# Shared Winograd sums carried from PSUM bank to PSUM bank by ScalarE instead of added by VectorE

## The chip, the cores and the metric

The kernel runs on one core of a Trainium2 chip. The engines that matter are TensorE (PE in the profile; PEld is its weight load), VectorE (DVE), ScalarE (ACT), GpSimd (POOL) and the DMA queue that SyncE (SP) feeds. The metric is device time in microseconds (us) of one execution.

## The reference

Attention with a block mask feeds a soft mixture of eight experts, which feeds a second network. The change lies in the mixture:

```python
for e in range(E):                       # E = 8, x is 2304 x 512
    h = np.maximum(x @ w1[e], 0.0)       # w1[e] is 512 x 1024
    ye = h @ w2[e]                       # w2[e] is 1024 x 512
    out += P[:, e:e + 1] * ye            # P from eight rounds of row and column scaling
```

Attention before it and the last network (matrix product, softmax, layer norm, matrix product) after it are the same in both kernels.

## The kernel before

Attention runs from the start to about 380 us, with expert 0 filled in between; the row and column scaling follows, and from 461 us the other seven experts run as fourteen units `u` = 2 to 15 (half an expert each). They run three times, for three blocks of 768 tokens. In **pass 0** (461 to 905 us) each unit's weights are also scaled, split into f16 high and low parts by ACT (high) and POOL (low) and stored; the second layer (`second_layer`) is a plain product. In **passes 1 and 2** (905 to 1690 us) the stored weights are read back, and the second layer (`second_products`) uses seven products as well. The last network runs from 1690 us to the end.

Every first layer (`first_layer`, 42 of them: 14 units in 3 passes) multiplies 2x2 blocks by Winograd's scheme: seven products 1 to 7, each for two halves `g` = 0, 1 of the hidden features. One product (`product`, L823 to L825) is six matmuls of 128x384 that accumulate in one PSUM bank. Bank a of a half takes products 1 and 2, bank b takes 6, 7 and 4, bank c takes 5 and 3. Sums that several outputs share are made outside PE: ACT copies product 1 out of bank a to SBUF (`r1`, L849), and DVE adds (`plus`, L835): u2 = b + r1 after product 6, u3 = b + r1 after 7, vu3 = c + u3 after 5, b + r1 in place after 4, and c + u2 in place after 3. Each finished output goes to `hidden`: in pass 0 ACT (L868) and DVE (L869) make the high and low parts of its ReLU, in passes 1 and 2 one DVE instruction (L880) makes the weighted ReLU into `hb`. From `hb`, ACT casts (`hf`, L887) and POOL subtracts (L888 the low part, L891 `minus` the differences; one `minus` of a unit runs on DVE), which feed the second products (`yps<-hf`). Results are added into `acc` by DVE (L935 in passes 1 and 2, L987 in pass 0).

First-layer banks and most of the second products' banks come from one pool of six (`l1p`); the second layer of pass 0 and every fourth second product use another pool of two (`mm`). A matmul that begins a bank's reuse waits until the engine that reads the old content is done. Two small matmuls, the squared norms of a coming unit's weights (`bound`, L488) and the steps of a table (`gate_table`, L523 to L544), write into unused columns of a first-layer bank (`aside`). A scheduler lays out each engine's order at build time from the program; at run time each engine works its list in that order.

## Time and profile before

| | |
|---|---|
| median of 3 runs | 1930.81 us (1930.1 to 1933.39) |
| profiled execution, its own time | 1930.03 us |
| span of its trace | 1928.1 us |
| PE busy over the span | 1815.9 us (94%) |
| DVE busy | 1469.4 us (76%) |
| ACT busy | 857.2 us (44%) |
| POOL busy | 1083.8 us (56%) |

The own time is the span plus 1.93 us around it. Busy times are sums over stages whose limits differ, so the two stages with first layers are read by themselves below. In rows of waits, the engine and line before the arrow waited, those behind it ended the wait; the numbers are us in total, times, and the longest in us. A matmul's recorded 0.33 us overlaps the next one's.

### The profile page before, as it was taken

To read this page: it belongs to the slowest core of one execution; us is meant where nothing else is said; L and a number is where in the kernel's file an instruction comes from. 1 tells how busy PE (TensorE), PEld (TensorE's weight loads), DVE (VectorE), ACT (ScalarE), POOL (GpSimd) and SP (SyncE) were. 2 spreads that over 40 slices of the span, in tenths; PEclk is the share of its full clock that TensorE was granted. 3 is DMA by queue.
4 is the path that set the end of the run, shared out by engine and by line. 5 is a ranking of instruction groups with operands and counts; after the bars stand their busy time and mean duration, and the time that the engine had idled before them with its cause. 6 is when DMAs were issued, how large, how long until landed. Compare 5 with 4: busy or idle time off the path is not lost.

```text
span 1928.1 us, 31148 instructions
## 1 busy us (share of the span) xinstructions
PE 1815.9 (94%) x10520; PEld 1218.5 (63%) x10520; DVE 1469.4 (76%) x3267; ACT 857.2 (44%) x1723; POOL 1083.8 (56%) x914
## 2 busy tenths in 40 slices
PE   4799999979999999999999999999999999999999
PEld 4688998877544454444566555665665555568887
DVE  6878777676787766676688788777778888889774
ACT  5676666574876757552422212223221221233332
POOL 7675655255777565651766747769564775841000
PEclk9899999989999999999999999999999999999999
DMA  8665645255585564452655555555555555451100
GB/s 230 160 173 141 172 128 163 83 178 160 201 269 191 199 202 162 148 196 67 200 178 156 171 166 161 158 144 179 164 158 177 157 169 169 157 205 49 39 23 33
DMA packets 191710, 300.47 MB, mean 156 GB/s; under 512 B 19760, under 2 KB 77760, under 8 KB 189632
## 3 DMA queue, kind: packets, MB, share of 16 engines
q1 hardware_dynamic: 191552, 298.49, 50.1%
q8 instruction: 84, 1.38, 0.3%
q14 instruction: 74, 0.61, 0.1%
HBM read 192.96 MB, written 77.14 MB: 140 GB/s over the span
## 4 chain that ended last, share of the span: by engine, by line
PE 39%; DVE 5%; POOL 3%; DMA 2%; issue 2%; ACT 0%; SPq 0%; DVEq 0%; POOLq 0%; ACTq 0%
PE yps L823 5%; PE yps L825 5%; PE yps L824 5%; PE psb L823 2%; PE psb L825 2%; PE psb L824 2%; PE ops L1290 2%; PE ops L1292 2%; PE ops L1291 2%; POOL hf L888 2%; PE h L1237 2%; PE h L1238 2%; PE h L1239 2%; PE psc L825 1%; PE psc L824 1%
## 5 line engine op out<-in xcount | busy, mean ns | idle before, releaser
L888 POOL TENSOR_TENSOR hf<-hb,hf 128x768 f16<-128x768 f32 x196 | 332.0, 1715 | 114.8 <-ACT hf L887 106.5
L887 ACT CAST hf<-hb 128x768 f16<-128x768 f32 x196 | 156.5, 830 | 331.8 <-POOL hb L891 130.2
L824 PEld LDWEIGHTS <-W 128*128 128x128 f16 x1960 | 192.5, 98 | 169.3 <-issue 43.8
L825 PEld LDWEIGHTS <-W 128*128 128x128 f16 x1960 | 192.7, 98 | 132.7 <-POOL W L554 3.0
L823 PEld LDWEIGHTS <-W 128*128 128x128 f16 x1960 | 192.5, 98 | 132.6 <-issue 3.6
L823 PE MATMUL yps<-hf,W 128*128 128x384 f16 x784 | 255.4, 326 | 1.8 <-POOL hf L888 1.7
L824 PE MATMUL yps<-hf,W 128*128 128x384 f16 x784 | 255.8, 326 | 0.0
L825 PE MATMUL yps<-hf,W 128*128 128x384 f16 x784 | 255.6, 326 | 0.0
L935 DVE SCALAR_TENSOR_TENSOR acc<-yps,rscw,acc 128x384 f32<-128x384 f32 x364 | 213.2, 608 | 14.4 <-PE yps L825 14.2
L823 PE MATMUL psb<-X,W 128*128 128x384 f16 x504 | 166.0, 329 | 12.0 <-DVE u L835 8.6
L825 PE MATMUL psb<-X,W 128*128 128x384 f16 x504 | 166.0, 330 | 0.7 <-POOL W L554 0.7
L824 PE MATMUL psb<-X,W 128*128 128x384 f16 x504 | 166.1, 330 | 0.0
L554 POOL TENSOR_TENSOR W<-raw,W 128x512 f16<-128x512 f32 x84 | 99.8, 1206 | 112.6 <-ACT W L553 108.4
L891 POOL TENSOR_TENSOR hb<-hb 128x768 f32<-128x768 f32 x84 | 155.6, 1852 | 5.9 <-DVE hb L880 5.4
L245 POOL TENSOR_SCALAR e<-e,sv 128x128 f32<-128x128 f32 (+2 forms) x144 | 82.9, 578 | 98.9 <-DVE sv L241 30.5
L981 PE MATMUL yps<-w,h 128*128 128x512 f16 x336 | 128.3, 382 | 10.7 <-DVE acc L987 9.5
L835 DVE TENSOR_TENSOR u<-psb,r 128x384 f32<-128x384 f32 x168 | 90.6, 551 | 60.0 <-PE psb L825 26.7
L554 POOL TENSOR_TENSOR w<-raw,w 128x512 f16<-128x512 f32 (+1 forms) x96 | 121.4, 1283 | 25.2 <-ACT w L553 24.9
L982 PE MATMUL yps<-w,h 128*128 128x512 f16 x336 | 128.2, 381 | 0.0
L983 PE MATMUL yps<-w,h 128*128 128x512 f16 x336 | 128.1, 381 | 0.0
L823 PE MATMUL psc<-X,W 128*128 128x384 f16 x336 | 110.2, 328 | 11.9 <-DVE acc L935 5.1
L1274 POOL TENSOR_SCALAR lh<-ln 128x1024 f16<-128x1024 f32 x18 | 19.1, 1062 | 176.9 <-DVE rs L1247 65.0
(262 smaller groups left out, 4700.4 us busy)
## 6 DMA issues: line engine op xcount, KB each, us to landing
W<-fd SPq DMA_DIRECT2D x392, 256.0 KB, 3.0
fd<-W SPq DMA_DIRECT2D x154, 256.0 KB, 2.2
raw<-in_w1s SPq DMA_DIRECT2D x14, 1024.0 KB, 6.1
raw<-in_w SPq DMA_DIRECT2D x14, 1024.0 KB, 7.4
fd<-w SPq DMA_DIRECT2D x84, 128.0 KB, 2.5
raw<-in_w SPq DMA_DIRECT2D x40, 256.0 KB, 3.6
kh<-khigh SPq DMA_DIRECT2D x64, 144.0 KB, 2.6
kl<-kraw SPq DMA_DIRECT2D x64, 144.0 KB, 2.7
```

Of the source, the lines that this page charges most:

```text
L554: nc.gpsimd.tensor_tensor(t[:, 1, :], raw, full(t[:, 0, :]), op=ALU.subtract)
L823: nc.tensor.matmul(ps, wh, xl, start=start and kc == 0, stop=False, skip_group_check=True)
L824: nc.tensor.matmul(ps, wh, xh, start=False, stop=False, skip_group_check=True)
L825: nc.tensor.matmul(ps, wl, xh, start=False, stop=stop and kc == 1, skip_group_check=True)
L835: nc.vector.tensor_tensor(to, bank[g, a], tmp[g, "r1" if a == "b" else name[1:]], op=ALU.add)
L887: nc.scalar.copy(hi, a)
L888: nc.gpsimd.tensor_tensor(lo, a, hi, op=ALU.subtract)
L891: eng.tensor_tensor(o, a, b, op=ALU.subtract)
L935: nc.vector.scalar_tensor_tensor(a, ps, r, a, op0=ALU.mult, op1=ALU.add)
L981: nc.tensor.matmul(ps, hl, ws[c][:, 0, :], start=c == 0, stop=False)
L982: nc.tensor.matmul(ps, hh, ws[c][:, 1, :], start=False, stop=False)
L983: nc.tensor.matmul(ps, hh, ws[c][:, 0, :], start=False, stop=c == 3)
```

## The change

Bank b of a half now begins as a copy of product 1: after product 1 ACT copies bank a into bank b (PSUM to PSUM), and products 6, 7 and 4 accumulate onto it, without a first matmul that clears. Bank b then holds u2 after product 6 and u3 after product 7, so ACT copies it out to SBUF twice, and after product 4 it is the finished output. DVE keeps only vu3 = c + u3 and c + u2. The products are issued in a written-out order in which the two halves alternate (1, 1, 5, 5, 6, 6, 2, 7, 2, 7, 4, 3, 4, 3). Since accumulation onto copied data needs banks that a matmul has written before, six matmuls write the six banks once before pass 0, and a chain of six one-column DVE instructions reads them. The steps of the table move to the two-bank pool, behind the first layer, and `bound` moves from behind product 5 to behind product 4 of the first half.

```diff
@@ -483,9 +483,9 @@
             if pin:
                 tc.keep_in_program_order(ins)
 
-    def bound(u, ps):
-
-        nc.tensor.matmul(ps, ones, norms.pop(u), start=True, stop=True)
+    def bound(u, ps, fresh=False):
+
+        nc.tensor.matmul(ps, ones, norms.pop(u), start=fresh, stop=True, skip_group_check=True)
         halved(tw[:, u, :], ps)
         k = powers[u] = sml.tile([P, 2], U32, tag="pw", name="pw")
         nc.vector.tensor_scalar(k, tw[:, u, :], -1.0, float(W1B + 189), op0=ALU.mult, op1=ALU.add)
@@ -515,19 +515,17 @@
         nc.vector.tensor_scalar_mul(w, pr[:, :, u // 2], rsc[:, u : u + 1])
         return w
 
-    table_bank = [None]
-
     def gate_table():
 
         gm = const.tile([P, 1], F32, name="pgm")
         nc.vector.tensor_reduce(gm, pr, axis=AX.XY, op=ALU.max)
         yield
-        pt = table_bank[0][:, BLK:512]
+        pt = mm.tile([P, 512], F32, tag="mm", name="pt")
         nc.tensor.transpose(pt[0:1, 0:P], gm, ident)
         g1 = const.tile([1, 1], F32, name="pg1")
         nc.vector.tensor_reduce(g1, pt[0:1, 0:P], axis=AX.X, op=ALU.max)
         yield
-        pb = table_bank[0][:, BLK:512]
+        pb = mm.tile([P, 512], F32, tag="mm", name="pt")
         nc.tensor.matmul(pb[:, 0:1], ones[0:1, :], g1, start=True, stop=True)
         k = const.tile([P, 1], U32, name="pk")
         c = const.tile([P, 1], U32, name="pc")
@@ -540,7 +538,7 @@
         yield
         pv = const.tile([P, P], F32, name="prt")
         for a, n in ((0, P), (P, NT * E - P)):
-            pt = table_bank[0][:, BLK:512]
+            pt = mm.tile([P, 512], F32, tag="mm", name="pt")
             nc.tensor.transpose(pt[0:n, 0:P], prs.rearrange("p t e -> p (t e)")[:, a : a + n], ident)
             nc.scalar.copy(pv[0:n], pt[0:n, 0:P])
             nc.sync.dma_start(pdram.rearrange("t e p -> (t e) p")[a : a + n], pv[0:n])
@@ -692,7 +690,7 @@
 
 
 
-    PRODUCTS = "1627543"
+    PRODUCTS = "1562743"
 
     SECOND = "3175624"
 
@@ -829,38 +827,43 @@
         bank, whole = {}, {}
         tmp = {}
 
-        def plus(g, name, a, to=None):
-            if to is None:
-                to = tmp[g, name] = tmpp.tile([P, BLK], F32, tag=name, name=name)
-            nc.vector.tensor_tensor(to, bank[g, a], tmp[g, "r1" if a == "b" else name[1:]], op=ALU.add)
+        def take(g, a):
+            whole[g, a] = l1p.tile([P, 512], F32, tag="l1", name=f"ps{a}")
+            bank[g, a] = whole[g, a][:, 0:BLK]
+
+        def plus(g, name, a, to):
+            nc.vector.tensor_tensor(to, bank[g, a], tmp[g, name], op=ALU.add)
             return to
 
-
-        plan = (("1", "a"), ("6", "b"), ("2", "a"), ("7", "b"), ("5", "c"), ("4", "b"), ("3", "c"))
-        for i, a in plan:
-            start, stop = i in "165", i in "243"
-            for g in range(2):
-                if start:
-                    whole[g, a] = l1p.tile([P, 512], F32, tag="l1", name=f"ps{a}")
-                    bank[g, a] = whole[g, a][:, 0:BLK]
-                product(W[i], X[i], bank[g, a], g, start, stop)
-                if i == "1":
-                    t = tmp[g, "r1"] = tmpp.tile([P, BLK], F32, tag="r1", name="r1")
-                    nc.scalar.copy(t, bank[g, "a"])
-                elif i == "6":
-                    plus(g, "u2", "b")
-                elif i == "2":
-                    hidden(g, 1, 1, bank[g, "a"])
-                elif i == "7":
-                    plus(g, "u3", "b")
-                elif i == "5":
-                    hidden(g, 2, 2, plus(g, "vu3", "c"))
-                elif i == "4":
-                    hidden(g, 2, 1, plus(g, "v", "b", bank[g, "b"]))
-                else:
-                    hidden(g, 1, 2, plus(g, "vu2", "c", bank[g, "c"]))
-            if i == "5" and aside:
-                aside(whole[0, "a"], whole[1, "a"])
+        def part(name):
+            return tmpp.tile([P, BLK], F32, tag=name, name=name)
+
+        plan = (
+            ("1", 0), ("1", 1), ("5", 0), ("5", 1), ("6", 0), ("6", 1), ("2", 0),
+            ("7", 0), ("2", 1), ("7", 1), ("4", 0), ("3", 0), ("4", 1), ("3", 1),
+        )
+        banks = {"1": "a", "2": "a", "6": "b", "7": "b", "4": "b", "5": "c", "3": "c"}
+        for i, g in plan:
+            a = banks[i]
+            if i in "15":
+                take(g, a)
+            product(W[i], X[i], bank[g, a], g, i in "15", i in "243")
+            if i == "1":
+                take(g, "b")
+                nc.scalar.copy(bank[g, "b"], bank[g, "a"])
+            elif i in "67":
+                t = tmp[g, "u2" if i == "6" else "u3"] = part("u2" if i == "6" else "u3")
+                nc.scalar.copy(t, bank[g, "b"])
+                if i == "7":
+                    hidden(g, 2, 2, plus(g, "u3", "c", part("vu3")))
+            elif i == "2":
+                hidden(g, 1, 1, bank[g, "a"])
+            elif i == "4":
+                hidden(g, 2, 1, bank[g, "b"])
+            elif i == "3":
+                hidden(g, 1, 2, plus(g, "u2", "c", bank[g, "c"]))
+            if (i, g) == ("4", 0) and aside:
+                aside(whole[1, "a"])
 
     def plain_hidden(hs):
         def hidden(g, i, j, src):
@@ -1075,7 +1078,7 @@
             norm(2)
             norm(3)
             for w in (2, 3):
-                bound(w, mm.tile([P, 512], F32, tag="mm", name="tot")[:, 0:2])
+                bound(w, mm.tile([P, 512], F32, tag="mm", name="tot")[:, 0:2], True)
         if i == 3:
             scale(2)
         if i == 4:
@@ -1086,6 +1089,13 @@
         while cost < 20:
             cost += next(begun, 20)
     run(begun)
+    fill6 = [l1p.tile([P, 512], F32, tag="l1", name="fill") for _ in range(6)]
+    for t in fill6:
+        nc.tensor.matmul(t[:, 0:BLK], ident16, X["1"][:, 0, 0, :], start=True, stop=True)
+    z = const.tile([P, 1], F32, name="z")
+    nc.vector.tensor_copy(z, fill6.pop()[:, 0:1])
+    while fill6:
+        nc.vector.tensor_tensor(z, fill6.pop()[:, 0:1], z, op=ALU.add)
     xctx.close()
     ectx = ExitStack()
     dec = ectx.enter_context(tc.tile_pool(name="dec", bufs=1, side="left"))
@@ -1123,17 +1133,16 @@
     for u in range(2, 16):
         hs = {}
 
-        def aside(first, second):
+        def aside(bank):
             for i, w in enumerate({2: (), 3: (4, 5)}.get(u, (u + 2,))):
                 if w < 16:
-                    bound(w, second[:, BLK + 2 * i : BLK + 2 * i + 2])
-            if 3 < u < 9:
-                table_bank[0] = first
-                next(table)
+                    bound(w, bank[:, BLK + 2 * i : BLK + 2 * i + 2])
 
         if u < 13:
             fetch(u + 3)
         first_layer(W, X, plain_hidden(hs), aside)
+        if 3 < u < 9:
+            next(table)
         if before:
             second_layer(*before)
         if u == 3:
```

The three places below are from the same first layer (pass 2, the eighth unit). A name such as psb_16746 is a tile with its number; the halves have their own tiles (before: psa_16728, psb_16746, psc_16795 for half 0; psa_16737 and psb_16755 for half 1. After: psa_16611, psb_16618, psc_16629 for half 0; psa_16620 and psb_16627 for half 1).

On PE, the first matmul of most products and of the second products between them (X1 is the input of product 1, and so on; a product is twelve rows, six weight loads and six matmuls), before:

```order
L823 MATMUL psa_16728<-X1_13157,W_16700 128x384
...
L823 MATMUL psa_16737<-X1_13157,W_16700 128x384
...
L823 MATMUL psb_16746<-X6_13158,W_16702 128x384
...
L823 MATMUL psb_16755<-X6_13158,W_16702 128x384
...
L823 MATMUL psc_16795<-X5_13161,W_16708 128x384
...
L823 MATMUL psa_16728<-X2_13159,W_16704 128x384
...
L823 MATMUL psb_16746<-X7_13160,W_16706 128x384
...
L823 MATMUL yps_16867<-hf_16578,W_16714 128x384
...
L823 MATMUL psb_16746<-X4_13162,W_16710 128x384
...
L823 MATMUL psc_16795<-X3_13163,W_16712 128x384
...
L824 MATMUL yps_16875<-hf_16578,W_16714 128x384
```

and with the change:

```order
L821 MATMUL psa_16611<-X1_13084,W_16583 128x384
...
L821 MATMUL yps_16773<-hf_16480,W_16599 128x384
...
L821 MATMUL psa_16620<-X1_13084,W_16583 128x384
...
L821 MATMUL psb_16618<-X6_13086,W_16587 128x384
...
L821 MATMUL psa_16611<-X2_13087,W_16589 128x384
...
L821 MATMUL psc_16629<-X5_13085,W_16585 128x384
...
L821 MATMUL psb_16618<-X7_13088,W_16591 128x384
...
L821 MATMUL yps_16746<-hf_16461,W_16597 128x384
...
L821 MATMUL psb_16618<-X4_13089,W_16593 128x384
...
L821 MATMUL psc_16629<-X3_13090,W_16595 128x384
...
L821 MATMUL yps_16754<-hf_16461,W_16597 128x384
...
L821 MATMUL psc_16636<-X3_13090,W_16595 128x384
```

Product 6 of half 0 (psb_16618 from X6) stands two groups of six matmuls behind the end of product 1 of that half, and the second product yps_16754, which takes the next bank in turn, the b bank of half 0, begins six matmuls after that bank's product 4 (psb_16618 from X4) has ended.

On ACT, the copies between the casts, before:

```order
L887 CAST hf_16373<-hb_16194 128x768
L887 CAST hf_16578<-hb_16448 128x768
L887 CAST hf_16597<-hb_16482 128x768
L553 CAST w32_16529<-f64_16539 128x256
L849 COPY r1_16735<-psa_16728 128x384
L849 COPY r1_16744<-psa_16737 128x384
L553 CAST w32_16546<-f64_16556 128x256
L887 CAST hf_16618<-hb_16616 128x768
L887 CAST hf_16638<-hb_16501 128x768
L887 CAST hf_16658<-hb_16482 128x768
```

and with the change:

```order
L890 CAST hf_16480<-hb_16359 128x768
L551 CAST w32_16412<-f64_16422 128x256
L853 COPY psb_16618<-psa_16611 128x384
L551 CAST w32_16429<-f64_16439 128x256
L853 COPY psb_16627<-psa_16620 128x384
L890 CAST hf_16501<-hb_16499 128x768
L856 COPY u2_16649<-psb_16618 128x384
L890 CAST hf_16521<-hb_16385 128x768
L856 COPY u2_16657<-psb_16627 128x384
L856 COPY u3_16673<-psb_16618 128x384
L890 CAST hf_16541<-hb_16359 128x768
L890 CAST hf_16560<-hb_16394 128x768
```

Two copies have become six, and they stand singly between casts of `hf` and of `w32` (the decoding of late weights), which come from POOL's and DVE's results.

On DVE, from the end of a decoding step on, before:

```order
L835 TENSOR_TENSOR u2_16753<-psb_16746,r1_16735 128x384
L835 TENSOR_TENSOR u2_16762<-psb_16755,r1_16744 128x384
L880 SCALAR_TENSOR_TENSOR hb_16770<-psa_16728,pb_16404 128x384
L880 SCALAR_TENSOR_TENSOR hb_16770<-psa_16737,pb_16404 128x384
L835 TENSOR_TENSOR u3_16785<-psb_16746,r1_16735 128x384
L835 TENSOR_TENSOR u3_16793<-psb_16755,r1_16744 128x384
L835 TENSOR_TENSOR vu3_16802<-psc_16795,u3_16785 128x384
L880 SCALAR_TENSOR_TENSOR hb_16804<-vu3_16802,pb_16404 128x384
L835 TENSOR_TENSOR vu3_16813<-psc_16806,u3_16793 128x384
L935 SCALAR_TENSOR_TENSOR acc_109<-yps_16867,rscw_106,acc_109 128x384
L880 SCALAR_TENSOR_TENSOR hb_16804<-vu3_16813,pb_16404 128x384
L835 TENSOR_TENSOR psb_16746<-psb_16746,r1_16735 128x384
```

and with the change:

```order
L883 SCALAR_TENSOR_TENSOR hb_16665<-psa_16611,pb_16291 128x384
L835 TENSOR_TENSOR vu3_16675<-psc_16629,u3_16673 128x384
L883 SCALAR_TENSOR_TENSOR hb_16665<-psa_16620,pb_16291 128x384
L883 SCALAR_TENSOR_TENSOR hb_16677<-vu3_16675,pb_16291 128x384
L938 SCALAR_TENSOR_TENSOR acc_109<-yps_16746,rscw_106,acc_109 128x384
L835 TENSOR_TENSOR vu3_16694<-psc_16636,u3_16692 128x384
L883 SCALAR_TENSOR_TENSOR hb_16703<-psb_16618,pb_16291 128x384
L883 SCALAR_TENSOR_TENSOR hb_16677<-vu3_16694,pb_16291 128x384
L835 TENSOR_TENSOR psc_16629<-psc_16629,u2_16649 128x384
L883 SCALAR_TENSOR_TENSOR hb_16712<-psc_16629,pb_16291 128x384
L894 TENSOR_TENSOR hb_16394<-hb_16394,hb_16359 128x768
L938 SCALAR_TENSOR_TENSOR acc_109<-yps_16754,rscw_106,acc_109 128x384
```

The two u2, two u3 and the two in-place additions on psb have gone; the weighted ReLU of psb_16618 stands behind vu3 of the other half.

## Rows read from the trace of the kernel before

**Rows 1.** The page: span, then busy us (share) and instructions of each engine.

```profile
span 1928.1 us, 31148 instructions
PE 1815.9 (94%) x10520; PEld 1218.5 (63%) x10520; DVE 1469.4 (76%) x3267; ACT 857.2 (44%) x1723; POOL 1083.8 (56%) x914
```

**Rows 2.** Windows: stretch, its us, busy of each engine, TensorE clock, DMA.

```profile
461.00:905.00 444.00, 417.54 (x2202) 216.91 (x2201) 329.92 (x587) 289.80 (x519) 265.92 (x217) 0.98 0.57 189
905.00:1690.00 785.00, 764.27 (x4635) 454.21 (x4634) 629.06 (x1131) 202.88 (x309) 515.98 (x317) 1.00 0.54 166
```

**Rows 3.** Waits of PE in pass 0 (461 to 905 us).

```profile
PE yps L981 <- DVE acc L987: 9.5, 10, 2.6
PE psc L823 <- DVE vu L835: 4.6, 6, 1.2
PE psa L531 <- DVE h L869: 2.6, 1, 2.6
PE psc L823 <- DVE h L869: 2.2, 1, 2.2
PE psa L825 <- POOL W L554: 1.5, 1, 1.5
```

**Rows 4.** Waits of PE in passes 1 and 2 (905 to 1690 us).

```profile
PE psb L823 <- DVE u L835: 7.6, 3, 3.7
PE psc L823 <- DVE acc L935: 5.1, 5, 1.8
PE psa L823 <- DVE acc L935: 2.3, 7, 0.5
PE psb L823 <- DVE acc L935: 2.0, 1, 2.0
PE psa L823 <- ACT r L849: 1.8, 5, 0.5
PE yps L823 <- POOL hf L888: 1.7, 1, 1.7
```

**Rows 5.** Windows of four stretches after long waits of PE, columns as in Rows 2.

```profile
540.00:600.00 60.00, 54.03 (x266) 27.63 (x264) 46.66 (x81) 42.66 (x76) 47.99 (x38) 0.91 0.71 236
660.00:670.00 10.00, 7.41 (x30) 3.10 (x28) 7.74 (x15) 10.00 (x18) 4.65 (x5) 0.83 0.53 164
1325.00:1345.00 20.00, 17.56 (x96) 9.93 (x96) 17.39 (x22) 6.93 (x12) 17.70 (x10) 0.91 0.60 197
1635.00:1645.00 10.00, 6.70 (x31) 3.62 (x31) 8.03 (x16) 2.72 (x5) 6.64 (x5) 0.83 0.47 137
```

**Rows 6.** Groups by line: the additions that go, and the copy.

```profile
L835 DVE TENSOR_TENSOR u<-psb,r 128x384 f32<-128x384 f32 x168 | 90.6, 551 | 60.0 <-PE psb L825 26.7 <-ACT r L849 25.4 <-ACT hf L887 7.4
L835 DVE TENSOR_TENSOR psb<-psb,r 128x384 f32<-128x384 f32 x84 | 46.4, 555 | 1.0 <-PE psb L825 0.8
L849 ACT COPY r<-psa 128x384 f32<-128x384 f32 x84 | 38.7, 477 | 34.6 <-PE psa L825 32.2 <-issue 2.3
```

**Rows 7.** Timeline of PE, two matmuls in a row (start, us).

```profile
1316.11 0.33 PE L824 MATMUL psa<-X,W 128*128 128x384 f16 x1
1316.27 0.33 PE L825 MATMUL psa<-X,W 128*128 128x384 f16 x1
```

**Rows 8.** Timeline of ACT: the copy after the matmul of Rows 7.

```profile
1316.69 0.48 ACT L849 COPY r<-psa 128x384 f32<-128x384 f32 x1 [2.83 <-PE psa L825]
```

**Rows 9.** Timeline of PE: the last matmul of another layer's product 1.

```profile
1006.31 0.33 PE L825 MATMUL psa<-X,W 128*128 128x384 f16 x1
```

**Rows 10.** Timeline of ACT behind it (idle before, and what ended it).

```profile
1009.37 0.83 ACT L887 CAST hf<-hb 128x768 f16<-128x768 f32 x1 [1.88 <-POOL hb L891]
1010.11 0.85 ACT L849 COPY r<-psa 128x384 f32<-128x384 f32 x2
```

**Rows 11.** Waits of ACT over the span: casts for POOL's differences.

```profile
ACT hf L887 <- POOL hb L891: 130.2, 58, 5.6
```

**Rows 12.** Timeline of DVE where pass 0 begins.

```profile
458.90 2.12 DVE L687 TENSOR_TENSOR y<-yps,y 128x384 f32<-128x384 f32 x4 [4.10 <-PE yps L680]
```

## The prediction

> **What bounds the kernel now.** I read the page first, then windows for the two stages that have first layers, then PE's waits in each, then the timeline at the places the change touches. Over the span PE is busy 94% [rows 1]; TensorE is the bound, and the change does not touch its matmuls. So nothing is won by freeing DVE as such: a gain can come only from time in which PE stands still. The windows give that time [rows 2]: in pass 0 PE is busy 417.5 of 444 us (26.5 idle), in passes 1 and 2 764.3 of 785 (20.7 idle). DVE is busy 74% and 80% there, ACT 65% and 26%. PE's waits say what ended the idle time. In pass 0 it is nearly always DVE [rows 3]: 9.5 us for `acc` (a bank of the two-bank pool not yet read), 4.6 for vu3, 2.2 for the c bank's old content, 2.6 for a table step that waits for the ReLU that still reads its bank. In passes 1 and 2 it is u (7.6 us in three waits) and `acc` (9.4 in three groups) [rows 4].
>
> A long wait costs twice. In the windows around the longest waits the granted clock is 0.91 and 0.83 [rows 5], that is, some matmuls after the wait run at the lower of the two levels, 1.2 in place of 2.4 GHz. The time lost is (1 - clock) times the window: 60 x 0.09 = 5.4, 10 x 0.17 = 1.7, 20 x 0.09 = 1.8, 10 x 0.17 = 1.7, together 10.6 us. Idle time and clock make 47.2 + 10.6 = 57.8 us: the ceiling of any gain in these stages.
>
> **What goes.** The 168 additions for u2 and u3 and the 84 in place on bank b: 90.6 + 46.4 = 137 us of DVE work [rows 6], 3.3 us in each of 42 first layers. ACT gets four more copies per layer (six for two), 168 x 0.477 = 80 us [rows 6]. No row shows an ACT copy from PSUM into PSUM. Its nearest rows are the copy to SBUF (0.477) and DVE's pair, which costs 0.551 into SBUF and 0.555 into PSUM: where the result goes makes no difference there. I take 0.48 and hold 0.55 possible; since the copy matters only by whether it beats the next product, 0.07 us changes no term below. (The Trainium skill, ScalarE: Activation LUTs, Step-by-step: what each stage is for, says that ScalarE writes PSUM with less latency than SBUF; by that the copy would be a little shorter and the sum the same. No run here shows it yet.)
>
> Pass 0. The waits for vu3 go: vu3 had to follow product 5 and, on a busy DVE, u3; now product 5 is early (60 matmuls ahead of product 3 of its half, where it was some 25), and one copy on ACT and one addition on DVE must fit between products 7 and 3, some 30 matmuls or 5 us apart in the new order: -4.6. The c bank is no longer taken behind DVE's backlog: -2.2. The table's matmuls leave the bank that ReLUs read: -2.6. The 9.5 us for `acc` are DVE's backlog of up to 2.6 us; 3.3 us of work per layer leave its queue, but not all stand ahead of the late `acc`, and the two-bank pool stays: I take half, -4.7 (bounds 0 and 9.5). The clock comes back where its wait goes: all of the 5.4 (the table's and the c bank's waits lie there) and half of the 1.7 after an `acc` wait: -6.2. Sum 20.3.
>
> Passes 1 and 2. The u waits go: product 7 now follows copies that ACT makes, and the two long waits (3.5 and 3.7 us) came while DVE was held by its own other work. -7.6, and the clock behind them, 1.8 + 1.7 = -3.5. Of 9.4 us for `acc` I take a third, -3.1, because the six banks are taken earlier in the new order. Sum 14.2.
>
> The 1.5 us for POOL's W, 1.7 for `hf` and 1.8 for ACT's r stay.
>
> **What comes.** First, a start-up: the six bank-writing matmuls need the banks of the last `yps`, whose four additions on DVE take 2.12 us from 458.90 on [rows 12], and the first product then waits for the chain of one-column reads. PE used to work through this stretch on products 1 and 6, 16 matmuls of 0.16 us [rows 7], 2.6 us. The next units' weights are late there anyway (the 1.5 us for W), which hides part: +2 (bounds 0 and 4).
>
> Second, ACT is now in PE's way. Undisturbed, a copy begins 0.42 us after the start of product 1's last matmul [rows 7, 8] and lasts 0.48: 0.9 us. In the layer shown, product 6 of the first half begins 13 matmuls after that start, 2.1 us; 1.2 to spare. In other layers there is more, 24 matmuls, and in pass 0 whole groups of second-layer matmuls stand between, which makes it 4 us and more in nearly all layers. But ACT is busy 65% there [rows 2], with 289.8 / 14 = 21 us of in-order work per layer and now 2 more, so some copies will come late: an estimate of 0.2 us per layer, +3 (bounds 0 and 10). In passes 1 and 2 the copy stands behind casts of `hf` that wait for POOL. One such case of before: product 1's last matmul starts at 1006.31 [rows 9], the cast waits 1.88 us for POOL until 1009.37, and the copy begins at 1010.11 [rows 10], 3.8 us behind instead of 0.42. Before, nothing but DVE's u noticed. Now product 6 would stand 4.3 - 2.1 = 2.2 us. Such waits are 58 in all, 2.2 us each [rows 11], two in each of the 28 layers. Also, the b bank of the first half is given to a second product six matmuls (1 us) after its product 4, while its ReLU on DVE (0.55) stands behind vu3 of the other half, which waits for a copy: no slack at all. If one layer in five is hit for the full 2.2 us, that is 0.4 us per layer, 28 x 0.4 = +11.2 (bounds 0 and 51, below).
>
> **Sum.** -20.3 - 14.2 + 2 + 3 + 11.2 = -18.3. The profiled execution took 1930.03 us, 0.8 below the median of the runs, which is nothing. 1930.0 - 18.3 = 1911.7, so 1912. The `acc` terms may give 8 us less or 11 more, the start-up 2 either way, the copies may cost 6 more or 11 less; as these hardly all fall to one side, I hold 13 us either way for this case: 1899 to 1925.
>
> **Rivals.** (A) *ACT's queue becomes the bound of the passes*: slower. If every layer of passes 1 and 2 has a copy behind a cast that waits 2.2 us for POOL and runs 0.83, less 1.2 to spare, it loses 1.8 us, 28 x 1.8 = 51; with 34.5 gained and 5 lost elsewhere that is +22, 1952. It decides against the change from (34.5 - 5) / 28 = 1.1 us per layer on. For it: 58 such waits, and single copies between casts in the new ACT order. Against it: in some layers of before the copy followed the matmul at once, as in rows 8; and when PE has once stood still, POOL catches up. (The Trainium skill, TensorE: Matmul & The Clock Gate, Architectural detail, says that ScalarE's and VectorE's queues are strictly first in, first out, and that PE pulls only weight loads ahead; so a blocked cast holds the copy and then every matmul behind product 6. Rows 10 agree, 3.8 us against 0.42.)
>
> (B) *The waits only move.* DVE stays late for `acc` and the b bank, and what u and vu3 gave is waited for there: the terms of "what goes" shrink to those for the table, c bank and clock of pass 0 (about 11) and the new ones eat them: 1930, no change. For it: `acc` is the largest wait already.
>
> (C) *All goes*: waits of DVE vanish whole and the copies are never late. 57.8 less the 5.0 that stay and 2 for the start-up is 51: 1879. For it: DVE falls from 74 to about 64% in pass 0.
>
> **Chances.** Forecast 0.62, A 0.18, B 0.12, C 0.08. A difference of 0.2% (3.9 us) is about what can be told from none; so faster 0.71 (forecast and C, with a little of the forecast's edge gone to no change and A), same 0.12, slower 0.17. The range that leaves out the far half of A and most of C is 1886 to 1942; the forecast's own is 1899 to 1925.
>
> **What would show it.** In the profile after: L835 down from 420 instructions (five per half and layer) to 168, L849's copies up from 84 to 252 at about 0.48 us; PE idle in pass 0 near 13 us in place of 26.5, with no wait for vu3 or in the table; in passes 1 and 2 no wait for u, and new rows of PE's psb waiting for ACT's copies, about 0.4 us per layer. A shows as such waits of 30 us and more in total; B as `acc` and ReLU waits that have grown. I would be wrong by the size of one term above all, the lateness of ACT's copies, which the order cannot tell.

## The result and the profile after

The changed kernel takes **1950.1 us** (median of 4 runs, 1947.28 to 1953.98) against 1930.45 of the kernel before beside it (1930.1 to 1933.39): ratio 1.0099, 95% interval 1.0087 to 1.0111. It is 1% slower where 1912 us and faster were forecast, and 1950 lies outside the range. The profiled execution took 1950.32 us, 20.3 more than that of before.

The page first, in the columns of [rows 1]:

```profile
span 1948.5 us, 30887 instructions
PE 1818.8 (93%) x10526; PEld 1221.0 (63%) x10526; DVE 1359.3 (70%) x3021; ACT 926.8 (48%) x1891; POOL 1088.5 (56%) x914
```

DVE is busy for 110 us less (137 us of additions left it) and ACT for 70 us more (80 us of copies came); PE's own work has hardly moved (1815.9 to 1818.8). So the 20 us are time in which PE stands still or runs at a lower clock. Four stages, cut at fixed events on PE's timeline (the last matmul of the row and column scaling, the last one of pass 0's second layer, the last second product, the last matmul of all), tell where:

| us | up to pass 0 | pass 0 | passes 1 and 2 | last network |
|---|---|---|---|---|
| before | 443.2 | 475.3 | 783.2 | 222.1 |
| after | 447.3 | 476.3 | 799.5 | 221.2 |
| difference | +4.1 | +1.0 | +16.3 | -0.9 |

The first stage holds the same work in both. Over all the kernels below it lasted 442.1 to 447.3 us, with the kernels that share its code on both ends, so +4.1 is the spread from one execution to the next and no effect of the change. What the change did is +1.0 in pass 0, where -15.3 was forecast (-20.3 + 2 + 3), and +16.3 in the passes, where -3.0 was (-14.2 + 11.2).

PE's waits after, first in pass 0 (461 to 905 us), to be held against [rows 3]:

```profile
PE yps L984 <- DVE acc L990: 11.2, 5, 3.2
PE psa L488 <- DVE h L872: 7.1, 5, 1.8
PE psc L821 <- DVE vu L835: 4.3, 3, 1.9
PE psa L821 <- DVE h L872: 2.2, 1, 2.2
PE psb L821 <- ACT u L856: 1.8, 2, 1.5
PE psb L821 <- ACT psb L853: 1.3, 1, 1.3
```

`acc` and vu3, which should have shrunk, stand where they were (9.5 and 4.6 before). The copies cost what was put down for them (3.1 us). New are 7.1 us in which `bound` (L488) waits for a ReLU. Then passes 1 and 2 (905 to 1690 us), to be held against [rows 4]:

```profile
PE psb L821 <- ACT psb L853: 11.1, 8, 3.0
PE yps L821 <- DVE acc L938: 6.9, 4, 2.4
PE yps L821 <- DVE hb L883: 4.0, 3, 2.1
PE psa L821 <- DVE acc L938: 3.9, 1, 3.9
PE yps L821 <- POOL hf L891: 3.0, 2, 2.0
PE psb L821 <- ACT u L856: 2.7, 3, 1.2
PE psc L821 <- DVE acc L938: 1.7, 2, 1.0
PE psc L821 <- DVE vu L835: 0.2, 1, 0.2
```

The u waits on DVE are gone (7.6 before). But `acc` waits are 12.5 us (9.4 before), `hb` is new with 4.0, and ACT's copies add 13.8. These rows sum to 33.5 us, those of [rows 4] to 20.5: +13.0. The clock adds the rest: summed over windows of 10 us from 915 to 1715, (1 - granted clock) times 10 us was 3.4 us before and 6.8 after. 13.0 + 3.4 = 16.4, the 16.3 of the table. In pass 0 (445 to 915) PE's idle time went from 26.5 to 29.5 us and the clock's loss from 6.8 to 5.1: +1.3, near the +1.0 of the table.

One late copy, in the passes. PE's timeline, the last matmul of product 1 and the first of product 6 (start, us, what it waited for):

```profile
1682.10 0.33 PE L823 MATMUL psa<-X,W 128*128 128x384 f16 x1
1685.07 0.32 PE L821 MATMUL psb<-X,W 128*128 128x384 f16 x1 [2.64 <-ACT psb L853]
```

and ACT's between the two:

```profile
1683.81 0.83 ACT L890 CAST hf<-hb 128x768 f16<-128x768 f32 x1 [1.88 <-POOL hb L894]
1684.55 0.85 ACT L853 COPY psb<-psa 128x384 f32<-128x384 f32 x2
```

ACT was free when product 1 ended, but the cast at the head of its list waited 1.88 us for POOL's difference, and the copies of both halves stood behind it. This is rival A's mechanism; it cost 8 waits, where A counted one in each of 28 layers.

`bound`, in pass 0: DVE's timeline ahead of the matmul, then PE's.

```profile
819.73 1.17 DVE L811 TENSOR_TENSOR raw<-s,raw 128x512 f32<-128x512 f32 x1
820.83 1.50 DVE L872 SCALAR_TENSOR_TENSOR h<-vu,h 128x384 f16<-128x384 f32 x1
822.26 0.55 DVE L872 SCALAR_TENSOR_TENSOR h<-psa,h 128x384 f16<-128x384 f32 x1
```

```profile
822.86 0.38 PE L488 MATMUL psa<-wq,ones 128*128 128x2 f32 x2 [1.82 <-DVE h L872]
```

A matmul of two columns holds PE for 1.82 us, because it writes beside bank a of half 1 and the ReLU that reads that bank stands in DVE's list behind a sum of the next unit's weights and another ReLU.

The groups by line, beside [rows 6]:

```profile
L835 DVE TENSOR_TENSOR vu<-psc,u 128x384 f32<-128x384 f32 x84 | 46.4, 553 | 94.1 <-ACT u L856 94.1
L856 ACT COPY u<-psb 128x384 f32<-128x384 f32 x168 | 78.4, 475 | 86.4 <-PE psb L823 86.0
L853 ACT COPY psb<-psa 128x384 f32<-128x384 f32 x84 | 39.0, 468 | 44.0 <-PE psa L823 41.4 <-DVE h L872 2.6
```

The copy from PSUM to PSUM takes 468 ns, the one to SBUF 475: the 0.48 us of the forecast. (The Trainium skill, ScalarE: Activation LUTs, Step-by-step: what each stage is for, has PSUM as the faster port for ScalarE. The rows agree in sign, by 7 ns of 475, which decides nothing here.)

### The profile page after: what moved, and what is told of

Same layout as the page of the kernel before. It is cut to its first block, busy times and chain, and to the rows that moved or that the text cites. A ratio compares the mean times of both kernels' runs of the same rounds, so it can differ in the third digit from the quotient of the medians.

```text
span 1948.5 us, 30887 instructions
## 1 busy us (share of the span) xinstructions
PE 1818.8 (93%) x10526; PEld 1221.0 (63%) x10526; DVE 1359.3 (70%) x3021; ACT 926.8 (48%) x1891; POOL 1088.5 (56%) x914
## 4 chain that ended last, share of the span: by engine, by line
PE 39%; POOL 6%; DVE 6%; issue 5%; DMA 2%; ACT 1%; SPq 0%; POOLq 0%; DVEq 0%; ACTq 0%
PE yps L821 4%; PE yps L822 4%; PE yps L823 4%; POOL hf L891 3%; PE psb L821 2%; PE psb L823 2%; PE psb L822 2%; PE ops L1299 2%; POOL hb L894 2%; PE ops L1301 2%; PE ops L1300 2%; PE h L1246 2%; PE h L1248 1%; PE h L1247 1%; DMA w<-in_w_in 1%
## 5 line engine op out<-in xcount | busy, mean ns | idle before, releaser
L821 PE MATMUL psb<-X,W 128*128 128x384 f16 x504 | 165.1, 328 | 16.9 <-ACT psb L853 12.5
L552 POOL TENSOR_TENSOR W<-raw,W 128x512 f16<-128x512 f32 x84 | 105.7, 1276 | 121.5 <-ACT W L551 115.1
L984 PE MATMUL yps<-w,h 128*128 128x512 f16 x336 | 128.8, 383 | 12.2 <-DVE acc L990 11.2
L856 ACT COPY u<-psb 128x384 f32<-128x384 f32 x168 | 78.4, 475 | 86.4 <-PE psb L823 86.0
L821 PE MATMUL psa<-X,W 128*128 128x384 f16 x336 | 110.5, 329 | 6.6 <-DVE acc L938 3.9
```

The lines of the kernel that those rows point to most:

```text
L552: nc.gpsimd.tensor_tensor(t[:, 1, :], raw, full(t[:, 0, :]), op=ALU.subtract)
L821: nc.tensor.matmul(ps, wh, xl, start=start and kc == 0, stop=False, skip_group_check=True)
L984: nc.tensor.matmul(ps, hl, ws[c][:, 0, :], start=c == 0, stop=False)
```

## Experiments

Theory of the time after the result: the loss of the passes is new waits of PE on engines that work their lists in order, and what pass 0 should have gained did not come since its waits are for DVE's backlog, which a few additions less don't end; `bound` costs pass 0 some us more. Rival: one piece of the change (ACT's queue, or `bound`) is the whole loss, and the rest pays as forecast. All runs in one table: the median, its ratio to the kernel before beside it with the 95% interval, and pass 0 and passes cut as above. "Moved" counts the matmuls, of the 4560 from the first second product to the last, that stand elsewhere in PE's list than before: after every edit the scheduler lays the lists out anew.

| run | median us | ratio | pass 0 | passes | moved |
|---|---|---|---|---|---|
| before | 1930.45 | | 475.3 | 783.2 | 0 |
| after | 1950.1 | 1.0099 (1.0087 to 1.0111) | 476.3 | 799.5 | 1232 |
| e1_bound_mm | 1941.28 | 1.0055 (1.0038 to 1.0072) | 471.0 | 803.1 | 1232 |
| e2_pass0_only | 1938.52 | 1.0041 (1.0026 to 1.0056) | 477.1 | 789.7 | 12 |
| e3_passes_only | 1946.9 | 1.0082 (1.0064 to 1.0101) | 473.7 | 799.5 | 1232 |
| e4_copies_on_dve | 1946.01 | 1.0081 (1.0066 to 1.0096) | 475.6 | 801.1 | 1249 |
| e5_order_only | 1940.82 | 1.0043 (1.0028 to 1.0058) | 475.1 | 793.0 | 702 |
| e6_sums_only | 1937.62 | 1.0025 (1.0016 to 1.0034) | 474.4 | 790.8 | 1045 |
| e7_distance | 1943.3 | 1.0055 (1.0039 to 1.0072) | 474.8 | 796.0 | 1122 |
| e8_table_apart | 1931.3 | 0.9995 (0.9986 to 1.0005) | 474.7 | 783.7 | 0 |
| e9_pass0_bound_mm | 1931.2 | 1.0005 (0.9996 to 1.0014) | 471.7 | 786.2 | 12 |
| e10_no_u_adds | 1939.39 | 1.0043 (1.0031 to 1.0056) | 474.2 | 791.4 | 674 |
| e11_no_copy_into_b | 1942.82 | 1.0059 (1.0045 to 1.0073) | 479.7 | 793.9 | 780 |
| e12_bound_early | 1930.49 | 1.0 (0.9991 to 1.0009) | 475.0 | 783.4 | 0 |
| e13_double_u_adds | 1932.81 | 1.0009 (1.0 to 1.0018) | 471.1 | 791.2 | 476 |
| e14_halved_boundary | 1936.16 | 1.0017 (1.0008 to 1.0026) | 475.0 | 786.8 | 6 |
| e15_swap_2_and_7 | 1932.79 | 1.0003 (0.9994 to 1.0012) | 476.3 | 786.5 | 108 |

Each ratio is formed from runs side by side; medians of different sets are not to be compared below 2 us (the kernel before had 1930.37 to 1932.3 in them). The stages are those of one execution each, and that execution can lie some us from the median: 3.3 above it in e1, 5.1 below it in e3, 5.1 above it in e13. In the passes the changed kernel, e1 and e3 have the same list of matmuls on PE, and so have e2 and e9, but their passes differ by 3.6 and by 3.5 us. So a difference of less than 4 us between two stages is not shown by this table alone.

Of the expectations printed below, five came out clearly in neither of their ranges (e4, e6, e10, e14, e15), and three miss the nearer one by 0.2 us (e5, e9, e11).

**Which stage, which part: e1 to e4.** `bound` in a bank of the two-bank pool (e1); the change in pass 0 alone, the passes with the old first layer (e2); in the passes alone (e3); the six copies of a layer on DVE (e4).

e1:

```diff
-                    bound(w, bank[:, BLK + 2 * i : BLK + 2 * i + 2])
+                    bound(w, mm.tile([P, 512], F32, tag="mm", name="tot")[:, 0:2], True)
```

e2 in the changed kernel, where `first_layer_old` is the function of before, and e3 in the kernel before, where `first_layer_new` is that of after (in e2, e3, e5, e7 and e9 the order of the weight loads, `PRODUCTS`, goes with the order of the products in the passes):

```diff
-            first_layer(W, X, hidden)
+            first_layer_old(W, X, hidden)
```

```diff
-            first_layer(W, X, hidden)
+            first_layer_new(W, X, hidden)
```

e4:

```diff
-                nc.scalar.copy(bank[g, "b"], bank[g, "a"])
+                nc.vector.tensor_copy(bank[g, "b"], bank[g, "a"])
...
-                nc.scalar.copy(t, bank[g, "b"])
+                nc.vector.tensor_copy(t, bank[g, "b"])
```

> The changed kernel with one edit: the norm matmul (bound) writes a bank of the two-bank pool instead of bank a of half 1, which a ReLU still reads. If the gain of pass 0 was eaten by PE waiting there for that ReLU (7.1 us in five waits in the changed kernel's trace), the time falls from 1950 to about 1942. If that wait only stands in for the next one (late acc or late ReLU parts on DVE), it stays at 1950 within 2 us.

> The change in pass 0 alone; passes 1 and 2 as before, with their old product order. If the loss lies in the passes, about 1930 (1926 to 1935). If pass 0 pays for start-up, table and bound, 1938 or more. If the gain that I forecast for pass 0 were real, 1915.

> The change in passes 1 and 2 alone; pass 0, bound and table as before, no bank-writing matmuls. If the loss lies in the passes, as the idle time of PE there says (34 us against 20.7, and the clock behind it), 1945 to 1952. If the two stages share it, 1938 to 1943.

> The changed kernel with all six copies of a first layer on DVE instead of ACT (order, banks and sums the same; DVE has eight instructions per layer for sums, where the kernel before had ten and two copies on ACT). Theory 1, copies stand in ACT's queue behind casts that wait for POOL: PE's 13.8 us of waits for ACT copies in the passes go, 1935 to 1940. Theory 2, the product order and the early reuse of the b bank cost the time, whoever copies: 1948 or more, and with DVE busier still, up to 1960.

e1: pass 0 falls from 476.3 to 471.0, and no wait of `bound` is left in it. PE's idle time there falls by 4.7 us at the same loss to the clock (5.1), so its place cost 5 us, near its 7.1 us of waits. e3: the passes come out at 799.5, as in the whole change, with pass 0 as before, so +16.3 does not need the new pass 0. e2: pass 0 keeps the loss to `bound`, and the passes, with their old code, still lengthen by 6.5 (below). e4: with the copies on DVE, PE's waits in the passes (920 to 1720 us) read

```profile
PE psb L821 <- DVE psb L853: 32.9, 14, 6.9
PE psb L821 <- DVE u L856: 1.7, 1, 1.7
PE yps L821 <- DVE hb L883: 0.9, 1, 0.9
```

No wait for `acc` or `hf` is left beside these: the three rows sum to 35.5 us, the eight of the changed kernel to 33.5, and the passes differ by 1.6. So with the copies elsewhere, one group of waits stands in for the others. That does not clear ACT's queue, since DVE's queue took its place; e11 below does better, as without the copy into bank b at all the passes still take 10.7 us more than before.

**Order and sums apart: e5, e6.** In the passes only: the new order of products with the old sums (e5), and the new sums in the old order (e6); pass 0 as before.

e5, against the new first layer:

```diff
-                nc.scalar.copy(bank[g, "b"], bank[g, "a"])
+                tmp[g, "r1"] = part("r1")
+                nc.scalar.copy(tmp[g, "r1"], bank[g, "a"])
...
-                nc.scalar.copy(t, bank[g, "b"])
+                tmp[g, t] = plus(g, "r1", "b", part(t))
...
-                hidden(g, 2, 1, bank[g, "b"])
+                hidden(g, 2, 1, plus(g, "r1", "b", bank[g, "b"]))
```

e6, against the new first layer:

```diff
-            ("1", 0), ("1", 1), ("5", 0), ("5", 1), ("6", 0), ("6", 1), ("2", 0),
-            ("7", 0), ("2", 1), ("7", 1), ("4", 0), ("3", 0), ("4", 1), ("3", 1),
...
+        plan = [(i, g) for i in "1627543" for g in range(2)]
```

> In passes 1 and 2 the new product order with the old sums (product 1 copied to SBUF, five additions per half on DVE, no copy into bank b); pass 0 as before. Theory 1 (the copy that PE must wait for costs the time): the order is harmless, 1928 to 1934. Theory 2 (the order and its reuse of banks cost it): 1941 or more, as with the whole change in the passes (1947).

> In passes 1 and 2 the new sums (bank b begins as ACT's copy of product 1, two copies out per half) in the old product order; pass 0 as before. Product 6 of a half then starts at least two groups of six matmuls behind product 1 of that half, as in the changed kernel. Theory 1: 1941 or more, with PE waiting some 10 us for the copies into bank b. Theory 2: 1928 to 1934.

Neither is innocent: the order costs 9.8 us in the passes, the sums 7.6, together 17.4 against 16.3. What PE waits for differs. e5 and then e6, PE's longest sums of waits from 905 to 1716 us:

```profile
PE yps L823 <- DVE hb L923: 13.6, 15, 2.0
PE psb L823 <- DVE acc L978: 8.6, 5, 2.4
```

```profile
PE psb L823 <- ACT psb L890: 10.6, 10, 1.8
PE psc L823 <- DVE acc L975: 6.2, 5, 2.8
PE yps L823 <- POOL hf L928: 4.9, 5, 1.5
```

With the order alone, a second product takes a first-layer bank before DVE's weighted ReLU has read it; with the sums alone, product 6 waits for ACT's copy.

**The copy's wait taken away: e7, e11.** e7 is e3 with the first matmul of product 6 pinned behind both products 5, so that at least 3.9 us of matmuls stand between products 1 and 6; e11 is the changed kernel without the copy into bank b.

e7, in `product` (`pin` is true for product 6):

```diff
+            if pin and kc == 0:
+                tc.keep_in_program_order(ins)
```

e11:

```diff
-                nc.scalar.copy(bank[g, "b"], bank[g, "a"])
...
-            product(W[i], X[i], bank[g, a], g, i in "15", i in "243")
+            product(W[i], X[i], bank[g, a], g, i in "156", i in "243")
```

> The change in passes 1 and 2 alone, with product 6's first matmul pinned behind both products 5, so that at least 24 matmuls (3.9 us) instead of 8 to 12 (1.3 to 1.95 us) lie between the end of product 1 and product 6 of a half. Theory 1 with the distance as the point: PE's waits for the copy (11 us in eight waits) fall under 3 us and the time from 1947 to 1934 to 1938. If PE stays late for other banks, it falls by less than 4 us.

> The changed kernel without the copy of product 1 into bank b: product 6 starts the bank afresh, so that u2, u3 and the sums on bank b lack product 1; the order of products, the copies of u and bound stay. If the waits of PE for that copy are what the passes lose (11.1 us there and 1.3 in pass 0), 1950 less 12 to 14: 1936 to 1938. If they only hold back a lateness that comes out elsewhere (as with product 6 pinned behind product 5), 1943 to 1948.

In e7 the wait of product 6 for the copy into bank b, 11.0 us in e3, is gone. Product 2, which writes the bank that the copy reads, now waits 3.5 us for the same copy (third row), so 7.5 us of waits for it left. PE's waits in the passes are now these:

```profile
PE psc L823 <- DVE acc L980: 10.9, 4, 5.1
PE yps L823 <- DVE hb L925: 6.8, 5, 3.9
PE psa L823 <- ACT psb L895: 3.5, 6, 0.8
```

The passes give back 3.5 us of these 7.5, which is within what one list shows in two executions; by the ratios it is 5 us. In e11 the passes give back 5.6 us of 11.1, and `bound`'s wait in pass 0 grows from 7.1 to 13.2 us. A wait removed by itself returned about half of itself; the rest was waited elsewhere.

**Pass 0: e8, e9, e12.** The kernel before with the table's steps in the two-bank pool (e8); the change in pass 0 alone with `bound` in the two-bank pool (e9); the kernel before with `bound` written behind product 7 instead of 5 (e12).

e8:

```diff
-        pt = table_bank[0][:, BLK:512]
+        pt = mm.tile([P, 512], F32, tag="mm", name="pt")
```

e9 is e2 with the edit of e1. e12, where `early` holds the call of `bound` that `aside` had:

```diff
+            if i == "7" and early:
+                early(whole[1, "a"])
```

> The kernel before with one part of the change: the table's steps in the two-bank pool, behind the first layer. The 2.6 and 0.7 us that PE waits for ReLUs there go, and the half-speed stretch behind the first of them: 1930.4 becomes 1924 to 1926. If the wait only moves to the two-bank pool, 1930.

> The change in pass 0 only, old first layers in passes 1 and 2, and bound in a bank of the two-bank pool. It tells what the new sums are worth in pass 0 once bound no longer stands in PE's way. Theory (waits only move: DVE's lateness stays when adds leave it): 1926 to 1931, no difference of more than 0.2% from the kernel before. Rival (the forecast of pass 0 was right but for bound and the start-up): 1930 less 20.3 plus 5, 1915.

> The kernel before with bound alone moved in the text from behind product 5 to behind product 7, so that 12 matmuls in place of 24 stand between the last product on its bank and bound. If the place of bound is what cost 7 to 9 us in the changed kernel, the same shows here: 1936 to 1939, and a wait of bound for the ReLU. If it cost only because ACT has more to do there, 1930 to 1933.

e8: the table's wait of 2.6 us [rows 3] is gone, the time is the same, and the wait for `acc` in pass 0 has grown from 9.5 to

```profile
PE yps L981 <- DVE acc L987: 12.6, 15, 2.7
```

e9: without `bound`'s wait, pass 0 is 3.6 us shorter than before, but not because PE waits less: it is idle 26.6 us there (26.5 before), and the whole gain is clock, a loss of 1.7 us against 6.8. e13, which gives DVE more to do, has as short a pass 0 (471.1). So no gain of the new sums is shown in pass 0. The passes, with 12 of 4560 matmuls moved, are 3.0 us longer: 1931.2, no change. One piece of that is a second product near the start of the passes that waits for POOL's `hf`: 1.75 us before, 3.38 in e2 and 3.40 in e9. The stretch of 40 us that holds it, in e2, in e9 and then before (columns as in [rows 2]):

```profile
920.00:960.00 40.00, 36.62 (x206) 20.84 (x205) 24.71 (x43) 17.38 (x29) 28.27 (x18) 0.92 0.66 210
```

```profile
920.00:960.00 40.00, 36.60 (x226) 21.95 (x225) 24.50 (x43) 18.18 (x31) 30.38 (x20) 1.00 0.64 200
```

```profile
917.00:957.00 40.00, 38.25 (x233) 22.68 (x232) 25.45 (x44) 18.05 (x31) 27.94 (x18) 1.00 0.66 216
```

Both are idle 1.6 us more than before, for the same code. In e2 the clock takes another 40 x 0.08 = 3.2 us; in e9 the same wait, in the same list of matmuls, cost no clock. e12 says nothing on the place of `bound`: in its trace only 16 of PE's 10520 matmuls stand elsewhere, and the scheduler put `bound` back where it was.

**DVE's load: e10, e13.** The kernel before with the additions for u2 and u3 left out, and with each of them done twice.

e10 (and the same for u3):

```diff
-                    plus(g, "u2", "b")
+                    tmp[g, "u2"] = tmp[g, "r1"]
```

e13, in `plus`:

```diff
+            for _ in range(2 if name in ("u2", "u3") else 1):
+                nc.vector.tensor_tensor(to, bank[g, a], tmp[g, "r1" if a == "b" else name[1:]], op=ALU.add)
```

> The kernel before with the additions for u2 and u3 left out: r1 stands in for both, so that vu2 and vu3 lack the products 6 and 7, and nothing else takes their place (no copies, no new order of products in the text). 168 additions, some 90 us, leave DVE. Theory (PE's waits are for DVE's in-order queue behind long work elsewhere, and freeing a few us per layer moves them only): 1922 to 1931. Rival (the forecast's reading, which took all waits for vu3 and u, half and a third of those for acc and the clock behind them as gone): 1930 less some 25 to 30, 1900 to 1905.

> The kernel before with each addition for u2 and u3 done twice: 168 additions, some 90 us, more on DVE, nothing else. If PE's waits measure how full DVE is (the forecast's reading), the new work shows as such: 90 us of which a good part lies in the layers where PE waits for u, acc and vu3, 1945 to 1965. If they measure long work that stands ahead in DVE's queue at a few places, and the order PE got, it costs no more than taking these additions away did: 1930 to 1942.

These two bear most on the question. The windows of e10 and then of e13, in the columns of [rows 2] (DVE is the third engine):

```profile
461.00:905.00 444.00, 417.84 (x2209) 218.38 (x2208) 305.48 (x531) 291.32 (x519) 262.15 (x217) 0.98 0.58 189
905.00:1690.00 785.00, 756.90 (x4583) 448.59 (x4581) 579.16 (x1007) 199.83 (x305) 508.76 (x312) 1.00 0.54 162
```

```profile
461.00:905.00 444.00, 417.42 (x2218) 218.28 (x2217) 360.73 (x648) 290.45 (x519) 262.12 (x217) 0.99 0.57 190
905.00:1690.00 785.00, 760.20 (x4609) 452.06 (x4608) 658.54 (x1235) 201.52 (x306) 510.10 (x314) 0.99 0.54 164
```

Against [rows 2] DVE does 24.4 and 49.9 us less in e10, 30.8 and 29.5 more in e13. Less work makes the kernel 0.43% slower, more work at most 0.18%. Both edits also moved 674 and 476 matmuls of the list, so they don't show what less or more work would do under an unchanged list. But by the forecast's reading e10 would have been 25 to 30 us faster; to hide that, its new list would have to cost 33 us and more, and no run here lost more than 20. (e13's stages are those of the slowest of its 11 executions.)

Where the u wait went: at the start of pass 2, in the 30th first layer, the step that closes pass 1 (L969) is on DVE's list. In the kernel before PE waits 3.46 us for u there, behind this:

```profile
1322.15 4.70 DVE L969 SCALAR_TENSOR_TENSOR acc<-y,cpi,acc 128x768 f32<-128x768 f32 x2
1326.77 1.01 DVE L835 TENSOR_TENSOR u<-psb,r 128x384 f32<-128x384 f32 x2
```

In the changed kernel no u is awaited there. In the same layer, behind the same step, a second product waits 2.08 us for the ReLU that frees its bank:

```profile
1338.09 5.03 DVE L972 SCALAR_TENSOR_TENSOR acc<-y,cpi,acc 128x768 f32<-128x768 f32 x2
1343.04 0.55 DVE L883 SCALAR_TENSOR_TENSOR hb<-psa,pb 128x384 f32<-128x384 f32 x1
```

```profile
1343.64 0.32 PE L821 MATMUL yps<-hf,W 128*128 128x384 f16 x1 [2.08 <-DVE hb L883]
```

In e10, with no u either, PE waits for vu in the same layer, 30 of its matmuls further on, with a later instruction of the same step ahead of vu on DVE:

```profile
1336.88 2.54 DVE L969 SCALAR_TENSOR_TENSOR acc<-y,cpi,acc 128x768 f32<-128x768 f32 x1 [0.79 <-POOL acc L950]
1339.35 1.98 DVE L880 SCALAR_TENSOR_TENSOR hb<-vu,pb 128x384 f32<-128x384 f32 x1
1341.25 0.54 DVE L835 TENSOR_TENSOR vu<-psc,r 128x384 f32<-128x384 f32 x1
```

```profile
1341.85 0.32 PE L823 MATMUL psc<-X,W 128*128 128x384 f16 x1 [3.60 <-DVE vu L835]
```

3.60 us for vu in place of 3.46 for u. (The Trainium skill, Perfetto Trace Analysis, Optimization Strategies, advises, where the idle matmul engine waits for others, to optimize the engines that block the critical path. Here that engine lost 168 instructions, and PE's idle time by the windows stayed in pass 0, 26.5 to 26.2 us, and grew in the passes, 20.7 to 28.1: at this place what counted was which instruction stood ahead of the awaited one.)

**What is left of the cause: e14, e15.** The step between passes in two halves, and products 2 and 7 exchanged in the kernel before (same sums, copies and loads).

e14:

```diff
-            v.scalar_tensor_tensor(s, y, cpi, s, op0=ALU.mult, op1=ALU.add)
+            for k in range(2):
+                v.scalar_tensor_tensor(s[:, k], y[:, k], cpi, s[:, k], op0=ALU.mult, op1=ALU.add)
```

e15:

```diff
-        plan = (("1", "a"), ("6", "b"), ("2", "a"), ("7", "b"), ("5", "c"), ("4", "b"), ("3", "c"))
+        plan = (("1", "a"), ("6", "b"), ("7", "b"), ("2", "a"), ("5", "c"), ("4", "b"), ("3", "c"))
...
-    PRODUCTS = "1627543"
+    PRODUCTS = "1672543"
```

> The kernel before with the last step between passes (acc plus y times cpi, 768 columns wide, four per pass boundary) in two halves of 384 columns, so that an addition for u has half as long a piece ahead of it. If the long u waits (3.46 and 3.71 us) are for that work, they shrink and the time falls by 2 to 6 us: 1924 to 1928. If the scheduler keeps both halves together, nothing changes: 1930 to 1932.

> The kernel before with products 2 and 7 exchanged and nothing else: same sums, same copies, same banks, same load on every engine, products in the order 1, 6, 7, 2, 5, 4, 3. It tells what another order costs by itself. If time goes with the load of the engines: 1929 to 1932. If it goes with how the order meets DVE's and ACT's queues: a change of 3 us or more, 1934 to 1945.

e14 is a miss: 1.0017, and the longest u wait became longer:

```profile
PE psb L823 <- DVE u L835: 10.8, 3, 6.5
```

The additions were not let in between the halves, and the halves did not take half as long. On DVE, ahead of that wait:

```profile
1324.86 8.04 DVE L970 SCALAR_TENSOR_TENSOR acc<-y,cpi,acc 128x384 f32<-128x384 f32 x4
```

8.04 us in place of 4.70 stand ahead of u, and PE waits 6.46 us in place of 3.46, with 6 matmuls of the list moved: the wait follows the work ahead of the awaited instruction. The time as a whole says less, +0.17%. e15: another order by itself, 108 matmuls moved, costs nothing that shows (1.0003), though single waits change places: `acc` in pass 0 is 17.7 us in it (9.5 before), u in the passes 4.0 (7.6 before).

## Why the prediction was wrong

**The step that failed** is "What goes": "Pass 0. The waits for vu3 go", with half of the `acc` waits and the clock, -20.3, and "Passes 1 and 2. The u waits go", -14.2. It took each wait of PE as a price that ends with the DVE instruction named in it. Term by term, in us of waits:

| term | forecast | measured |
|---|---|---|
| pass 0, vu3 | -4.6 | -0.3 (4.6 to 4.3) |
| pass 0, bank taken behind a ReLU | -2.2 | 0 (on bank c before, on bank a now) |
| pass 0, table | -2.6 | -2.6, but `bound` +7.1 |
| pass 0, `acc` | -4.7 | +1.7 |
| pass 0, clock | -6.2 | -1.7 |
| pass 0, start-up | +2 | +0.3 (first product, for the chain of reads) |
| pass 0, copies | +3 | +3.1 |
| pass 0, other waits (POOL's W, ACT's W and `r`, u, ReLUs) | 0 | -6.4 |
| passes, u | -7.6 | -7.6 |
| passes, `acc` | -3.1 | +3.1 |
| passes, `hb` | 0 | +4.0 |
| passes, clock | -3.5 | +3.4 |
| passes, copies | +11.2 | +13.8 |
| passes, other waits (`r`, `hf`, vu) | 0 | -0.3 |

The rows sum to -15.3 forecast and +1.2 measured in pass 0, and to -3.0 and +16.4 in the passes. The clock rows are those of one execution each. The waits that were to stay did not: POOL's W (1.5) and ACT's `r` (1.8) went, `hf` grew from 1.7 to 3.0.

The costs of the copies, the part that the text called most doubtful, were sized well: +14.2 forecast, +16.9 measured. The u waits went in the changed kernel, as forecast. But -7.6 was no gain: the text itself noted that the two long ones "came while DVE was held by its own other work", and that work stays. The changed kernel itself shows it at one of the two: the same step held DVE, and PE waited 2.08 us there for a ReLU instead of u. e14 shows it from the other side, 3.0 us more wait behind a step 3.3 us longer. In e8 the table's wait goes and the time stays, and e7 returns half of the copy's. For the whole, e10 and e13 speak against DVE's amount of work as what sets the waits, 74 us less in the two windows at +0.43% and 60 us more at +0.09%, though both also changed the list.

**A term that was missing:** the move of `bound`. It was described with the change and not costed. Behind product 4 of the first half it meets the ReLU of bank a, half 1, while that stands in DVE's list; e1 puts its price at 5 us in pass 0. A second one is `hb`, +4.0 in the passes: that a second product takes a bank before its ReLU has run was noted for the b bank, without a price of its own.

**The rivals.** (B), the waits only move, is the one whose mechanism the runs bear out (the changed kernel, e7, e8, e14), but its number, 1930, let the new waits only eat the gains. (A) named the number, 1952, by a mechanism that is real and too small: waits for copies are 13.8 us, not 30 and more, and e6, which has the copies without the order, loses less than half of the whole in the passes (7.6 of 16.3). That its number is near 1950 is luck. In the two stages together 18.7 us of waits went and 34.6 came: 16.9 for copies, which the forecast itself had priced nearly so, 7.1 for `bound`, 4.8 for `acc`, 4.0 for `hb`, 1.8 others.

**What stays open.** How the 9.8 us of the new order divide into its own waits and the mere loss of the old order; e5 and e6 had their lists laid out anew too, so that their sum, 17.4, comes near 16.3 is no proof that the two add up. In the table the passes lengthen with the matmuls moved: 783.2 to 783.7 at none, 786.2 to 789.7 at 6 to 108, 790.8 to 803.1 above 400, and this holds for e10 and e13 as well, whose loads on DVE differ by over 130 us. Since the kernels that move more also change more, it is a correlation. e14 comes nearest to more work under an unchanged list; no run takes much work from DVE without moving hundreds of matmuls. None of the runs beats the kernel before.

## What to carry to other kernels

A row "PE waits for X" names the last instruction of a chain, not its cause: before counting the wait as a gain, read on that engine's timeline what stood ahead of X, and ask what is awaited there once X is gone. On engines that work a list in order, a small matmul or copy that is moved is priced at its new place by the reader of its bank, however short it is itself. Where a scheduler lays out the lists, leave out the suspected work and double it, each in one run, before building the change: if both leave the time or worsen it, the engine's load alone does not set it. Count beside it how much of the list the edit moved, and compare two executions of one list before reading a small difference between stages.

## What was not expected of the hardware

The prediction's "A long wait costs twice" holds in some cases only: the clock does not follow the length of a wait. The same second product waited 3.38 us in e2 and 3.40 in e9, in the same list of matmuls; the granted clock over the 40 us around it was 0.92 and 1.00, so one wait cost 3.2 us more than the other. Summed over the passes, the clock took 3.4 us before, 6.8 after and 8.5 in e2 and e14. The largest, 11.9 and 10.2 us, are in e1 and e4, whose passes are the longest, but e1 has the list of the changed kernel there, with its 6.8. So what the clock gives back for a wait that goes is no fixed amount.

A DVE instruction is not a fixed amount of time either. In the kernel before, one 768-column instruction of the step between passes took 2.39 us on average at 1322, while POOL worked without a break; the last three, after POOL's work had ended at 1710.9, took 1.00 us each, among them these two:

```profile
1713.20 1.93 DVE L969 SCALAR_TENSOR_TENSOR acc<-y,cpi,acc 128x768 f32<-128x768 f32 x2
```

In e14 the halves took 2.0 to 2.15 us at 1325 and 0.60 at the end. The weighted ReLU of vu, 1.06 us on average before, took 1.29 in e10 and 0.90 in e13, which is part of why DVE was busy for only 71 us less in e10, where 90.6 us of additions left. Where POOL was idle it took 0.55 us in all four kernels looked at (before, after, e10, e13). What POOL does to these instructions no run takes apart.
